# Staging the queries of an attention block in one step of 128 partitions, with 24 crossing transfers in place of 12, and a new order table

## The chip, the cores and the metric

One core of a Trainium2 chip runs one program with five instruction streams: TensorE (PE in the profile, with its weight loads as PEld), VectorE (DVE), ScalarE (ACT), GpSimd (POOL) and SyncE (SP). SP only issues DMAs here, all of the kernel's. Each stream is executed in the order in which it was written; the streams wait for each other through semaphores. The metric is device microseconds of one execution. The kernel before takes 738.09 us (median of 3 runs, 735.95 to 739.26).

## The reference

```python
def _A_ref(x, wqkv, wo):            # x: 1 x 2048 x 512
    H = 32; Dh = D // H; W = 256    # 32 heads of 16, window of 256
    qkv = (x @ wqkv).reshape(B, S, 3, H, Dh) ...
    scores = jnp.einsum("bhqd,bhkd->bhqk", q, k) * (Dh ** -0.5)
    mask = (idx[:, None] - idx[None, :] >= 0) & (idx[:, None] - idx[None, :] < W)
    p = _softmax(jnp.where(mask, scores, -1e9), axis=-1)
    o = jnp.einsum("bhqk,bhkd->bhqd", p, v)
    return o ... @ wo
def _B_ref(x, w_gate, w_up, w_down):    # 512 -> 1376 -> 512
    return (_sigmoid(x @ w_gate) * (x @ w_up)) @ w_down

h = x + _A_ref(_layernorm(x), wqkv, wo)
h2 = h + _B_ref(_layernorm(h), w_gate, w_up, w_down)
```

Layernorm, attention over a causal window of 256 positions, a projection and a residual, then a second layernorm and a gated unit with its own residual. All of it is float32 data; the kernel multiplies float16 halves (a high and a low part) three times for one product, so that the result keeps nearly float32 accuracy.

## The kernel before

**Stages.** The 2048 rows are cut into 8 blocks of 256 (b = 0 to 7). Attention runs from the start to about 430 us, block after block, several blocks under way at once; the gated unit runs over 8 pairs of row tiles and fills TensorE from about 450 us to the end. Its weights are read, split into halves and combined during the attention, on DVE, ACT and POOL, written to DRAM (`wr<-chunk`) and read back into place when the attention's buffers come free.

**What one block does.** `do_ln` normalizes two row tiles (`normal`: statistics and `rs`, the scaled variance, on DVE at L585; `rs` to the power of -1/2 on POOL at L588; the scaling on DVE) and transposes them. `do_qk` multiplies by the query and key weights (L406) into a PSUM tile of the ring `mm`, which has two buffers, and evacuates it into a staging tile: a scaled high half (ACT or DVE, helper at L359 or L363) and then the low half, product less high half, on DVE at L720. `do_queries` (L745) and `do_keys` move the staged halves with DMAs across partitions into `SQ` and `SK`, the operands of the score products. `do_s` (L799) computes scores of a pair of heads for one row maximum each, `row_max` on DVE takes it (L784); the maxima go back through a transpose and two small DMAs (`mh`, `mt`, L811 and L815) into `SQ` as extra rows. `do_st` (L853, L854, L855, L864) computes the transposed scores, ACT takes the exponential (L829), POOL cuts the triangles (L837, L842), `do_pv` (L890) multiplies by the values, ACT or DVE and DVE evacuate (`RH`), a DMA transpose and POOL bring the rows back (`RT`, `OS`), and `do_wo` multiplies by the output weights (L406).

**The staged queries.** Query columns are packed so that a row of a staging tile holds data for one of two positions, u = 0 or 1, beside each other in the stacked operand `SQ`: partitions 0 to 63 belong to u = 0, 64 to 127 to u = 1, and the other position has to hold zeros. The staging tile `sq` therefore has a place for both u in each row, was set to zeros once, and the evacuation writes 64 partitions to their u = 0 places in one instruction and the other 64 to their u = 1 places in a second one. For each of the 16 evacuations (8 blocks, two each) this makes two high-half and two low-half instructions. For each of 4 pairs of heads p, three DMAs (c = 0, 1, 2: the high half twice, the low half once) then pick every fourth partition, 32 rows of 4096 bytes each, 12 transfers a block.

**What sets the order.** Every operation is a step of a generator; the list `ORDER` names, step by step, which generator goes on and on which of the allowed engines. It was found by a search beforehand. A step that can run on one of several engines (the high halves, the subtractions) takes the one that the number names. So the table fixes the stream of each engine word for word, SP's with all DMAs too, and a transfer stands in SP's queue behind whatever the table put ahead of it.

Of the kernel before, what the change touches and what calls it, by code (L numbers as in the profile page):

```python
# [35 lines left out]
P = 128  # L36
# [300 lines left out]
def tile_block(ctx, tc, x, wqkv, wo, wg, wu, wd, out):  # L337
# [119 lines left out]
    for i in range(2):  # L457
        (G if i else V).memset(stage[i][0].rearrange("p h j i u t -> p (h j i u t)").bitcast(F32), 0.0)
# [1104 lines left out]
```

## Time and profile before

| | |
|---|---|
| median of 3 runs | 738.09 us |
| profiled execution, its own time | 739.39 us |
| its span, first to last instruction | 737.6 us |
| DVE busy | 621.1 us |
| ACT busy | 465.7 us |
| POOL busy | 368.7 us |
| TensorE clock granted | 1.00 of full speed throughout |
| DMA issues on SP | 538 |

The profiled execution lies 1.30 us above the median. Busy time is the union of an engine's records. A matmul's record starts when it starts, but its end is modelled, so that matmuls that follow each other overlap in the records; short waits between two of them do not show as idle time. "Idle before" in a row is the time in which the engine did nothing before these instructions, and the arrow names what ended it. DMA-issuing instructions of SP have durations, but are not counted as busy.

### The profile page before, as it was taken

Reading aid. Unit: us, or ns where it says so; the run is one execution under the profiler, and the core shown is the slowest. Engines: PE = TensorE matmul, PEld = TensorE weight load, DVE = VectorE, ACT = ScalarE, POOL = GpSimd, SP = SyncE. Lnnn points to the kernel's source line nnn. Section 1 sums busy time; section 2 is a strip of 40 time slices with the busy share of each in tenths; the row PEclk is TensorE's granted clock in tenths of the full one; section 3 lists DMA queues with packets and bytes.
Section 4 is the critical chain, followed back from the end, with each engine's and each line's share of the span. In section 5 each row is a group of like instructions: output and inputs, shape, how many; then the busy total and the mean of one; then the engine's idle time right before and its main releaser. Section 6 shows DMA issues by size and latency. Waiting matters only on the chain.

```text
span 737.6 us, 19193 instructions
## 1 busy us (share of the span) xinstructions
PE 723.5 (98%) x7008; PEld 501.8 (68%) x7008; DVE 621.1 (84%) x1870; ACT 465.7 (63%) x846; POOL 368.7 (50%) x451
## 2 busy tenths in 40 slices
PE   9999999999999999999999899999999999999997
PEld 5686877777776777786665454576666565766476
DVE  8999999998999999999999889986486767675752
ACT  5967989778898877899788777643233333233320
POOL 2553656545656574666685443455432544344250
PEclk9999999999999999999999999999999999999999
DMA  8797784978648878669889999866537575545453
GB/s 312 185 245 229 176 188 115 183 189 162 174 125 168 184 188 191 161 186 183 233 186 212 256 253 300 192 117 137 95 80 135 102 143 94 113 93 97 93 131 102
DMA packets 216031, 123.63 MB, mean 168 GB/s; under 512 B 174912, under 2 KB 189504, under 8 KB 215936
## 3 DMA queue, kind: packets, MB, share of 16 engines
q1 hardware_dynamic: 215936, 122.40, 72.2%
q8 instruction: 55, 0.90, 0.5%
q14 instruction: 40, 0.33, 0.2%
HBM read 46.17 MB, written 21.92 MB: 92 GB/s over the span
## 4 chain that ended last, share of the span: by engine, by line
PE 85%; DVE 5%; DMA 4%; ACT 3%; issue 2%; POOL 0%; SPq 0%; DVEq 0%; ACTq 0%; POOLq 0%
PE mmp L406 18%; PE sp L1201 15%; PE mmp L1378 12%; PE pvp L890 9%; PE sp L799 8%; PE stp L1201 7%; PE pvp L1201 3%; PE stp L864 3%; PE stp L854 3%; PE stp L853 2%; PE stp L855 2%; PE mmp L700 1%; PE mmp L1384 1%; DVE junk L784 1%; DMA wr<-chunk 1%
## 5 line engine op out<-in xcount | busy, mean ns | idle before, releaser
L784 DVE CUSTOM_DVE_ANT_0 junk<-sp,mask 128x320 uint8<-128x320 f32 (+4 forms) x512 | 215.8, 464 | 16.5 <-PE sp L799 13.8
L829 ACT ACTIVATE pa<-stp,kappa 128x512 f32<-128x512 f32 (+1 forms) x256 | 154.2, 645 | 28.3 <-PE stp L855 25.5
L1201 PEld LDWEIGHTS <-x 128*128 128x128 f16 x1008 | 98.1, 98 | 87.6 <-DMA x<-hl 0.9
L799 PE MATMUL sp<-SK,SQ 96*128 96x192 f16 (+3 forms) x960 | 127.5, 232 | 1.6 <-DVE mq L784 0.8
L799 PEld LDWEIGHTS <-SQ 96*128 96x128 f16 x960 | 79.6, 97 | 28.1 <-issue 9.7
L406 PE MATMUL mmp<-xT,W 128*128 128x256 f16 x672 | 97.1, 272 | 0.3
L829 ACT ACTIVATE pb<-stp,kappa 128x512 f32<-128x512 f32 x128 | 82.9, 686 | 18.0 <-PE stp L864 16.5
L1201 PE MATMUL sp<-W,x 128*128 128x512 f16 (+1 forms) x420 | 88.2, 349 | 0.0
L837 POOL TENSOR_SCALAR_AFFINE_SELECT pa<-pa 128x1024 f32<-128x1024 f32 x56 | 62.2, 1111 | 31.9 <-ACT pa L829 31.9
L359 ACT ACTIVATE SQ<-SQ 128x512 f16<-128x512 f32 (+3 forms) x65 | 34.0, 534 | 57.5 <-DVE SQ L1285 13.0
L406 PEld LDWEIGHTS <-W 128*128 128x128 f16 x672 | 60.5, 97 | 8.2 <-DVE sq L720 0.6
L842 POOL TENSOR_SCALAR_AFFINE_SELECT pb<-pb 128x512 f32<-128x512 f32 x64 | 41.2, 645 | 45.1 <-ACT pb L829 45.0
L890 PE MATMUL pvp<-pa,VT 128*17 128x128 f32 (+1 forms) x1408 | 62.5, 307 | 0.0
L854 PE MATMUL stp<-SQ,SK 100*128 100x256 f16 x224 | 59.6, 270 | 0.0
L366 POOL TENSOR_TENSOR SQ<-SQ,SQ 128x512 f16<-128x512 f32 (+3 forms) x41 | 38.5, 945 | 38.3 <-DVE SQ L361 21.3
L855 PE MATMUL stp<-SQ,SK 100*128 100x128 f16 x256 | 55.4, 218 | 0.4 <-ACT pb L829 0.3
L842 POOL TENSOR_SCALAR_AFFINE_SELECT pa<-pa 128x512 f32<-128x512 f32 x64 | 41.5, 652 | 23.5 <-ACT pa L829 23.3
L890 PEld LDWEIGHTS pvp<-pa,VT 128*17 128x17 f32 x1408 | 37.7, 97 | 22.7 <-issue 3.3
L406 PE MATMUL mmp<-WO,oT 128*128 128x512 f16 x192 | 51.0, 379 | 1.1 <-DMA oT<-whl 0.8
L853 PE MATMUL stp<-SQ,SK 100*128 100x128 f16 x224 | 49.2, 220 | 2.6 <-ACT pa L829 1.8
L406 PE MATMUL mmp<-W,xT 128*128 128x512 f16 x192 | 49.7, 378 | 0.0
L864 PE MATMUL stp<-SQ,SK 100*128 100x256 f16 x256 | 47.4, 272 | 1.2 <-ACT pa L829 1.2
(231 smaller groups left out, 1506.4 us busy)
## 6 DMA issues: line engine op xcount, KB each, us to landing
SQ<-sq SPq DMA_DIRECT2D x96, 128.0 KB
wr<-chunk SPq DMA_DIRECT2D x28, 256.0 KB
SK<-mem SPq DMA_DIRECT2D x16, 384.0 KB
chunk<-in_wd_dram SPq DMA_DIRECT2D x20, 256.0 KB
X<-in_x_dram SPq DMA_DIRECT2D x16, 256.0 KB
mem<-sk SPq DMA_DIRECT2D x8, 512.0 KB
out_dram<-X SPq DMA_DIRECT2D x16, 256.0 KB
W<-wr SPq DMA_DIRECT2D x7, 512.0 KB
```

The lines of the kernel that those rows point to most:

```text
L406: PE.matmul(ps, a_of(a, k), b_of(b, k), start=(k == 0 and i == 0), stop=(k == n - 1 and i == 2))
L784: V.tensor_tensor_reduce(out=junk[:, c0:], in0=ps[:, c0:], in1=mask[:, c0:], scale=1.0, scalar=-3.0e38, op0=ALU.add, op1=ALU.max, accum_ou ...
L799: PE.matmul(ps[:, col:col + k1 - k0], q, SK[0:96, (2 * a + hf) % 5, 4 * (p % 2) + j, k0:k1], start=True, stop=True)
L829: S.activation(dst, a, AF.Exp, scale=kappa)
L842: G.affine_select(out=p, in_=p, pattern=[[0, 4], [1, 128]], compare_op=ALU.is_ge, fill=0.0, base=0, channel_multiplier=-1)
L853: PE.matmul(a[:, 0:128], ks(k0, g, j), qs(b, g, j, 0, 128), start=True, stop=True)
L854: PE.matmul(a[:, 128:384], ks(k0 + 1, g, j), qs(b, g, j, 0, 256), start=True, stop=True)
L855: PE.matmul(a[:, 384:512], ks(k0 + 3, g, j), qs(b, g, j, 128, 256), start=True, stop=True)
L864: PE.matmul(a[:, u, :], ks(k0 + 2, g, j + u), qs(b, g, j + u, 0, 256), start=True, stop=True)
L890: PE.matmul(ps[32 * j:32 * j + 17, u, q0:q1], VT[:, kt % 6, 8 * j + g, :], w[:, j, c:c + q1 - q0], start=first, stop=last, skip_group_chec ...
L1201: PE.matmul(ps, X2[p % 2][part][:, (a * COUNT[part] + at) * 2 + k, :], operand(c, j)[:, b, k, :], start=first and k == 0 and i == 0, stop= ...
L1378: PE.matmul(ps, hT[p, c, r][:, a, half * kinds[c] + i, :], W["d"][2 * c + i][:, b, j, :], start=fresh and c == 0 and i == 0 and n == 0, st ...
```

## The change

The staging tile becomes one flat row of 64 + 2 x 2048 elements a partition. All 128 partitions are evacuated by one instruction a half, always to the u = 0 place of the row's second part (from element 64 on). The place for u is now made by the transfer: for u = 0 it reads 2048 elements from element 64 of the row, for u = 1 from element 0, so that the same data appear 64 elements later, behind zeros. Each transfer takes 16 rows, and there are 24 a block in place of 12; the bytes stay the same.

```diff
-        stage[i] = pool.tile([P, 2, 4, 4, 2, 64], F16, name=f"sq{i}"), ...
+        stage[i] = pool.tile([P, 64 + 4 * 2 * 512], F16, name=f"sq{i}"), ...
...
-        times = 2 - c
...
         if c:
...
         else:
-            parts = [(ps[64 * u:64 * u + 64].rearrange("r j (i t) -> r j i t", t=64),
-                      [dst[64 * u:64 * u + 64, h, 2 * jj:2 * jj + 2, :, u, :] for h in range(2)],
-                      sc["x" + nm][64 * u:64 * u + 64] if raw else float(2.0 ** -20)) for u in range(2)]
-        for x, (hi, _), f in parts:
-            copy(hi, x, f)
+            src = ps.rearrange("r j (i t) -> r (j i) t", t=64)
+            hi, lo = (dst[:, 64:].rearrange("r (h s u t) -> r h s u t", h=2, u=2, t=64)[:, h, 8 * jj:8 * jj + 8, 0, :] for h in range(2))
+        copy(hi, src, f)
...
-        for x, (hi, lo), f in parts:
-            V.scalar_tensor_tensor(lo, x, f, hi, op0=ALU.mult, op1=ALU.subtract)
+        V.scalar_tensor_tensor(lo, src, f, hi, op0=ALU.mult, op1=ALU.subtract)
...
         for c in range(3):
-            nc.sync.dma_start(SQ[b % 2][32 * c:32 * c + 32, 4 * p:4 * p + 4]...,
-                              stage[int(b == 1)][0][p:P:4, c // 2]...)
+            at = 64 + c // 2 * 2048
+            for u in range(2):
+                nc.sync.dma_start(SQ[b % 2][32 * c + 16 * u:32 * c + 16 * u + 16, 4 * p:4 * p + 4]...,
+                                  stage[int(b == 1)][0][64 * u + p:64 * u + 64:4, at - 64 * u:at - 64 * u + 2048])
```

Two smaller edits come with it. In `normal`, all row tiles but the first two compute `rs` on POOL, just ahead of the power that was there before. And the last low half made from a loaded weight chunk may now be made on POOL too, as a scaling in place and a subtraction:

```diff
-        V.tensor_scalar(rs, mv[:, 1:2], EPS, float(2.0 ** -shift), op0=ALU.add, op1=ALU.mult)
+        if early:
+            V.tensor_scalar(rs, mv[:, 1:2], EPS, float(2.0 ** -shift), op0=ALU.add, op1=ALU.mult)
...
+        if not early:
+            G.tensor_scalar(rs, mv[:, 1:2], EPS, float(2.0 ** -shift), op0=ALU.add, op1=ALU.mult)
         G.tensor_tensor(out=rs, in0=rs, in1=nhalf, op=ALU.pow)
...
+    def rest(lo, x, w, hi):
+        if plan.on == POOL_:
+            G.tensor_scalar(x, x, w, None, op0=ALU.mult)
+            subtract(lo, x, hi)
+        else:
+            V.scalar_tensor_tensor(lo, x, w, hi, op0=ALU.mult, op1=ALU.subtract)
...
 ORDER = [
-    3203, 7427, 7427, 7427, 771, 6659, 3331, 1027, 7811, 640, ...
```

The new table chooses POOL for four such low halves. TensorE executes the same 7008 matmuls in nearly the same order; the other streams are reordered throughout.

The first place shown is DVE's stream at the first of the two query evacuations of block 7. `sq_119` is the staging tile, `mmp` the PSUM tile of the product, `chunk<-X,sg` a low half of a gate weight, `junk,mq` a row maximum (an instruction and the read of its result). Before:

```order
L1088 SCALAR_TENSOR_TENSOR chunk<-X,sg,chunk 128x512
L720 SCALAR_TENSOR_TENSOR sq_119<-mmp,sq_119 64x8x64 x2
L1088 SCALAR_TENSOR_TENSOR chunk<-X,sg,chunk 128x512
L784 ISA junk,mq<-sp,mask 128x320
L784 ISA mq 128x1
```

The same place in DVE's stream of the changed kernel, where the table also put the high half on DVE (`whl` is a half of the attention's output):

```order
L368 TENSOR_SCALAR sq_119<-mmp 128x8x64
L366 CAST whl<-OS 128x512
L792 ISA junk,mq<-sp,mask 128x320
L792 ISA mq 128x1
L726 SCALAR_TENSOR_TENSOR sq_119<-mmp,sq_119 128x8x64
```

Two low halves of 64 partitions became one of 128, and the two weight halves that stood around them stand elsewhere.

The second place is SP's stream in block 6, around the last query transfers (`SQ_73<-sq_119`) of its first pair of heads; `SK<-mem` brings keys, `oT<-whl` and `RT<-RH` are transposes of the attention's output, `wr<-chunk` writes split weights. Before:

```order
L745 DMA SQ_73<-sq_119 32x2048
L736 DMA SK<-mem 96x2048
L745 DMA SQ_73<-sq_119 32x2048 x2
L666 DMA_TRANSPOSE oT<-whl 128x8x128
L745 DMA SQ_73<-sq_119 32x2048
L1099 DMA wr_5270<-chunk 256x1x512
L1099 DMA wr_5849<-chunk 256x1x512
L745 DMA SQ_73<-sq_119 32x2048
L1099 DMA wr_5882<-chunk 256x1x512
L745 DMA SQ_73<-sq_119 32x2048 x2
L913 DMA_TRANSPOSE RT<-RH 128x8x128
```

The same stretch of SP's stream in the changed kernel:

```order
L753 DMA SQ_73<-sq_119 16x2048 x2
L742 DMA SK<-mem 96x2048
L1121 DMA wr_5742<-chunk 256x1x512
L753 DMA SQ_73<-sq_119 16x2048
L675 DMA_TRANSPOSE oT<-whl 128x8x128
L753 DMA SQ_73<-sq_119 16x2048
L1121 DMA wr_5290<-chunk 256x1x512
L753 DMA SQ_73<-sq_119 16x2048 x8
L921 DMA_TRANSPOSE RT<-RH 128x8x128
L1121 DMA wr_5106<-chunk 256x1x512
```

Between the keys and the transpose `RT<-RH`, 10 half-size transfers stand where 6 stood; the last three of the first pair are among the eight in a row.

More of the change, by code (lines that the diff above doesn't have):

```diff
@@ L455, in tile_block @@
     for i, pool in enumerate((qk, wp)):
-        stage[i] = pool.tile([P, 2, 4, 4, 2, 64], F16, name=f"sq{i}"), pool.tile([P, 2, 4, B], F16, name=f"sk{i}")
+        stage[i] = pool.tile([P, 64 + 4 * 2 * 512], F16, name=f"sq{i}"), pool.tile([P, 2, 4, B], F16, name=f"sk{i}")
     for i in range(2):
-        (G if i else V).memset(stage[i][0].rearrange("p h j i u t -> p (h j i u t)").bitcast(F32), 0.0)
+        (G if i else V).memset(stage[i][0].bitcast(F32), 0.0)
     V.tensor_copy(identh, ident)
@@ L576, in normal @@
     def normal(t, key, ring, tile, shift, n_of=1, ln1=False):
-        e, n = yield {DVE_: 1.0}, key, ["ln"]
+        early = ln1 and t < 2
+        e, n = yield {DVE_: 1.0 if early else 0.87}, key, ["ln"]
         src = xs[t][0] if ln1 else home(t)
@@ L584, in normal @@
         rs = small.tile([P, 1], F32, name="rs")
-        V.tensor_scalar(rs, mv[:, 1:2], EPS, float(2.0 ** -shift), op0=ALU.add, op1=ALU.mult)
+        if early:
+            V.tensor_scalar(rs, mv[:, 1:2], EPS, float(2.0 ** -shift), op0=ALU.add, op1=ALU.mult)
         both = "xn" in C["alts"]
-        e, = yield {POOL_: 1.1 if both else 0.62}, [e]
+        e, = yield {POOL_: 1.1 if both else 0.62 if early else 0.75}, [e]
+        if not early:
+            G.tensor_scalar(rs, mv[:, 1:2], EPS, float(2.0 ** -shift), op0=ALU.add, op1=ALU.mult)
         G.tensor_tensor(out=rs, in0=rs, in1=nhalf, op=ALU.pow)
@@ L705, in do_qk @@
                 mm3(ps[:, j, :], lambda a, k: W1[:, a, k, c0:c0 + P], lambda a, k: xT[b][:, a, k, :], k, KT)
-        times = 2 - c
-        e, = yield alt("qk", ACT_, ACT=0.52 * times + 0.16 * (times - 1), DVE=0.62 * times + 0.16 * (times - 1)), [e] + ["xq"] * raw
+        e, = yield alt("qk", ACT_, ACT=0.52, DVE=0.62), [e] + ["xq"] * raw
+        f = sc["xq"] if raw else float(2.0 ** -20)
         dst = stage[int(b == 1)][c]
         if c:
-            parts = [(ps, [dst[:, h, 2 * jj:2 * jj + 2, :] for h in range(2)], sc["x" + nm] if raw else float(2.0 ** -20))]
+            src, hi, lo = ps, *(dst[:, h, 2 * jj:2 * jj + 2, :] for h in range(2))
         else:
-            parts = [(ps[64 * u:64 * u + 64].rearrange("r j (i t) -> r j i t", t=64),
-                      [dst[64 * u:64 * u + 64, h, 2 * jj:2 * jj + 2, :, u, :] for h in range(2)],
-                      sc["x" + nm][64 * u:64 * u + 64] if raw else float(2.0 ** -20)) for u in range(2)]
-        for x, (hi, _), f in parts:
-            copy(hi, x, f)
-        e, = yield {DVE_: 0.63 * times + 0.157 * (times - 1)}, [e]
+            src = ps.rearrange("r j (i t) -> r (j i) t", t=64)
+            hi, lo = (dst[:, 64:].rearrange("r (h s u t) -> r h s u t", h=2, u=2, t=64)[:, h, 8 * jj:8 * jj + 8, 0, :] for h in range(2))
+        copy(hi, src, f)
+        e, = yield {DVE_: 0.63}, [e]
         plan.free("mm", n, e)
-        for x, (hi, lo), f in parts:
-            V.scalar_tensor_tensor(lo, x, f, hi, op0=ALU.mult, op1=ALU.subtract)
+        V.scalar_tensor_tensor(lo, src, f, hi, op0=ALU.mult, op1=ALU.subtract)
         plan.mark(("qk", b, c, jj), e)
@@ L743, in do_queries @@
         for c in range(3):
-            e, = yield {DMA_: 0.645}, needs, [], 0.85
-            nc.sync.dma_start(SQ[b % 2][32 * c:32 * c + 32, 4 * p:4 * p + 4].rearrange("r j i u t -> r j (i u t)"),
-                              stage[int(b == 1)][0][p:P:4, c // 2].rearrange("r j i u t -> r j (i u t)"))
+            at = 64 + c // 2 * 2048
+            for u in range(2):
+                e, = yield {DMA_: 0.645}, needs, [], 0.42
+                nc.sync.dma_start(SQ[b % 2][32 * c + 16 * u:32 * c + 16 * u + 16, 4 * p:4 * p + 4].rearrange("r j i u t -> r (j i u t)"),
+                                  stage[int(b == 1)][0][64 * u + p:64 * u + 64:4, at - 64 * u:at - 64 * u + 2048])
         plan.mark(("queries", b, p), e)
@@ L1009, in do_amax, with lower, halves @@
             plan.mark(("scale", nm), t)
-    def halves(hi, lo, x, w, cols, needs):
+    def lower(cols, last):
+        costs = dict(DVE=Port(cols / 960 + 0.13))
+        if last:
+            costs["POOL"] = Port(2 * (cols * 0.0021 + 0.1))
+        return costs
+    def rest(lo, x, w, hi):
[4 more added lines that the diff above has]
+            V.scalar_tensor_tensor(lo, x, w, hi, op0=ALU.mult, op1=ALU.subtract)
+    def halves(hi, lo, x, w, cols, needs, last):
         t, = yield alt("phi", ACT_, ACT=cols / 1200 + 0.187, DVE=Port(cols / 1920 + 0.075)), needs
         copy(hi, x, w)
-        t, = yield {DVE_: Port(cols / 960 + 0.13)}, [t]
-        V.scalar_tensor_tensor(lo, x, w, hi, op0=ALU.mult, op1=ALU.subtract)
+        t, = yield lower(cols, last), [t]
+        rest(lo, x, w, hi)
         return t
@@ L1028, in do_split @@
             hi, lo = (W["l"][:r, h, :] for h in range(2))
-            t = yield from halves(hi, lo, x, sc["sd"][:r], D, [t])
+            t = yield from halves(hi, lo, x, sc["sd"][:r], D, [t], True)
             plan.free("chunk", place, t)
@@ L1045, in part @@
             hi, lo = (W["d"][m][:, h, j:j + n, :].rearrange("p j n -> p (j n)") for h in range(2))
-            t = yield from halves(hi, lo, x, sc["sd"], n * HALF, needs)
+            t = yield from halves(hi, lo, x, sc["sd"], n * HALF, needs, last is not None)
             plan.mark(("dpart", m, j), t)
@@ L1086, in part @@
             copy(hl[:, 0, :], x[i], sc[scale])
-            t, = yield {DVE_: Port(cols / 960 + 0.13)}, [t]
-            V.scalar_tensor_tensor(hl[:, 1, :], x[i], sc[scale], hl[:, 0, :], op0=ALU.mult, op1=ALU.subtract)
+            t, = yield lower(cols, last is not None), [t]
+            rest(hl[:, 1, :], x[i], sc[scale], hl[:, 0, :])
             plan.mark(("part", c, k, j), t)
```

449 rows, old and new, of the table ORDER are left out of this document.

## The prediction

> **What bounds the kernel now.** I read the head of the page, then the windows of the span, then TensorE's waits, then the groups of instructions by shape, and last SP's own timeline, because that is where the change adds work.
>
> ```profile
> span 737.6 us, 19193 instructions
> PE 723.5 (98%) x7008; PEld 501.8 (68%) x7008; DVE 621.1 (84%) x1870; ACT 465.7 (63%) x846; POOL 368.7 (50%) x451
> ```
>
> TensorE is busy for 723.5 of 737.6 us, so 14.1 us is all of its visible idle time. Where it lies is read from the windows; the columns are the stretch, its length, the busy us of PE, PEld, DVE, ACT and POOL with their instructions, the granted clock, the DMA engines' share and GB/s.
>
> ```profile
> 0.00:25.00 25.00, 23.36 (x97) 15.84 (x98) 21.41 (x52) 17.03 (x37) 7.92 (x16) 1.00 0.79 265
> 25.00:50.00 25.00, 23.32 (x207) 17.83 (x206) 24.22 (x93) 19.82 (x40) 16.42 (x20) 1.00 0.85 219
> 75.00:100.00 25.00, 24.28 (x311) 19.22 (x310) 24.24 (x106) 22.16 (x54) 14.65 (x21) 1.00 0.72 174
> 350.00:375.00 25.00, 24.61 (x342) 16.47 (x341) 24.00 (x82) 18.62 (x32) 16.72 (x21) 1.00 0.79 211
> 375.00:400.00 25.00, 23.27 (x290) 15.84 (x287) 24.38 (x88) 21.50 (x36) 16.36 (x21) 1.00 0.95 208
> 400.00:425.00 25.00, 22.26 (x241) 12.95 (x239) 21.46 (x42) 18.98 (x34) 13.95 (x17) 1.00 1.01 240
> 425.00:450.00 25.00, 24.07 (x176) 11.72 (x175) 22.94 (x42) 17.89 (x31) 10.48 (x12) 1.00 1.11 268
> 700.00:737.60 37.60, 33.80 (x283) 27.34 (x280) 16.32 (x32) 5.93 (x11) 10.86 (x13) 1.00 0.47 114
> ```
>
> The idle time of a window is its length less PE's busy time: 1.64 and 1.68 us in the first two, 0.72 at 75, then 0.39, 1.73, 2.74 and 0.93 from 350 to 450, and 3.80 in the last stretch. These make 13.6 of the 14.1. So the middle of the attention and the gated unit are bound by TensorE itself at a clock of 1.00, and the change, which adds and takes no matmul, can gain only in the first 50 us, around 75 to 100, and from 350 to 450, where the attention runs out while the gated unit's weights are still being made. The last 38 us hold nothing that it touches. One reserve: matmul ends are modelled, so short waits hide in the busy time; the visible 14.1 is a lower bound of what TensorE waits.
>
> What ended the idle time, by name (engine, result, line, what was waited for: us, times, longest):
>
> ```profile
> PE stp L853 <- ACT pa L829: 1.8, 2, 1.6
> PE stp L864 <- ACT pa L829: 1.2, 2, 1.0
> PE mmp L659 <- ACT xT L359: 1.1, 1, 1.1
> PE mmp L406 <- DMA oT<-whl: 0.8, 1, 0.8
> PE stp L853 <- ACT pb L829: 0.6, 2, 0.4
> PE stp L855 <- ACT pb L829: 0.3, 1, 0.3
> PEld L406 <- DVE sq L720: 0.6, 2, 0.3
> ```
>
> The exponentials on ACT (`pa`, `pb`) make 1.8 + 1.2 + 0.6 + 0.3 = 3.9 us. Of the low half that this change halves, only 0.6 us in two places is waited for directly.
>
> **The change part by part.** First the staging.
>
> ```profile
> L720 DVE SCALAR_TENSOR_TENSOR sq<-mmp,sq 64x512 f16<-64x512 f32 x28 | 19.2, 687 | 0.5 <-ACT sq L359 0.2
> L720 DVE SCALAR_TENSOR_TENSOR sk<-mmp,sk 128x512 f16<-128x512 f32 x14 | 9.5, 679 | 0.0
> L720 DVE SCALAR_TENSOR_TENSOR sq<-mmp,xq,sq 64x512 f16<-64x512 f32 x4 | 3.0, 750 | 0.1
> L359 ACT ACTIVATE sq<-mmp 64x512 f16<-64x512 f32 x28 | 16.5, 589 | 4.1 <-PE mmp L406 3.4 <-PE sp L799 0.6
> L359 ACT ACTIVATE sq<-mmp,xq 64x512 f16<-64x512 f32 x4 | 2.7, 682 | 1.4 <-DVE xq L398 1.3
> L359 ACT ACTIVATE sk<-mmp 128x512 f16<-128x512 f32 x12 | 7.0, 596 | 3.8 <-PE mmp L406 3.3 <-PE sp L799 0.2
> ```
>
> The keys show the price of the new form: 128 partitions take 679 ns where 64 take 687, and 596 against 589 on ACT. Halving the number halves the time. On DVE 32 low halves (19.2 + 3.0 = 22.2 us) become 16 (14 x 0.679 + 2 x 0.750 = 11.0): **-11.2 us**. On ACT 32 high halves (16.5 + 2.7 = 19.2 us) become 13, since the table puts 3 on DVE: at 0.596, 7.7 us, **-11.5 us**; DVE gets those 3 back, about +1.8 at the same price (estimate from ACT's row).
>
> ```profile
> L585 DVE TENSOR_SCALAR rs<-mv 128x1 f32<-128x1 f32 x32 | 4.9, 153 | 1.1
> L588 POOL TENSOR_TENSOR rs<-rs,nhalf 128x1 f32<-128x1 f32 x32 | 19.3, 602 | 33.0 <-DVE rs L585 32.9
> L1088 DVE SCALAR_TENSOR_TENSOR chunk<-X,sg,chunk 128x512 f16<-128x512 f32 x20 | 15.8, 804 | 0.0
> L366 POOL TENSOR_TENSOR X<-X 128x512 f32<-128x512 f32 x7 | 9.1, 1303 | 12.2 <-DVE X L1107 12.2
> ```
>
> Thirty of 32 `rs` leave DVE: 30 x 0.153 = 4.6 us, of which 14 (2.1 us) belong to the attention. Four weight low halves leave it too: 4 x 0.804 = 3.2 us. With them DVE loses 11.2 + 2.1 + 3.2 - 1.8 = 14.7 us before the end of the attention; but the new table puts value evacuations and weight halves on DVE that were on ACT or POOL, about ten of 0.6 (the 0.596 of ACT's row again), some 6 us. So **DVE's net is about -9 us**. POOL gains 30 small operations, whose price is not in the trace: above 0.153 (DVE's) and below 0.602 (the power of one column on POOL). I take 0.4, nearer to the POOL row, 12 us over the whole program; and 4 x 2 operations of 512 columns at up to 1.3, 10 us. POOL is busy for 50%, and in the windows from 350 on at most 16.7 of 25. Its new `rs` waits for the statistics where the power waited for `rs` before, so nothing new stands behind a wait: the triangles queued behind it, and `do_pv` behind those, wait no longer than by the operation itself. I cost POOL at nothing; if that cover goes, one layernorm in the open costs 0.6 at most, and the two weight halves that could meet a triangle 2.6: the end is +3.
>
> **What of it reaches the end.** DVE is busy for 24.0 and 24.4 of 25 us between 350 and 400, and 24.2 in both early windows, so microseconds taken from it are carried forward rather than lost in its own gaps. ACT idles for 3.5 to 7 us in each of the windows from 350, so that most of what is taken from it before 330 us, where its last query half stands, is lost in gaps ahead of the place at which TensorE waits for it.
> - First 50 us: the 1.1 us wait for `xT` (a copy on ACT) follows two early high halves saved (2 x 0.682), but those stood behind 1.3 us of waiting for `xq`. I take **-0.3**, ends 0 and -1.1.
> - Direct waits for the low half: one of the two instructions goes, **-0.5** of the 0.6.
> - DVE's 9 us in 350 to 450: idle there and at 75 is 0.72 + 0.39 + 1.73 + 2.74 + 0.93 = 6.5, less ACT's 3.9 leaves 2.6. I take **-2.5**. Ends: 0, if DMAs are what is late; -9.0, if all of DVE's relief lay on the path through hidden short waits.
> - ACT: a quarter of 3.9, **-1.0**; ends 0 and -3.9 (contained in DVE's -9.0, as both act on one place).
>
> Then what it adds: DMA issues.
>
> ```profile
> L745 SPq DMA_DIRECT2D SQ<-sq x96: 467/589/1725, 19.4 to 345.9; - x96
> SQ<-sq SPq DMA_DIRECT2D x96, 128.0 KB
> SK<-mem SPq DMA_DIRECT2D x16, 384.0 KB
> 356.92 3.91 DMA SK<-mem
> 282.61 1.20 SPq L815 DMA_DIRECT2D SQ<-mt  x2
> 289.04 1.11 SPq L745 DMA_DIRECT2D SQ<-sq  x2
> 298.19 1.26 SPq L913 DMA_TRANSPOSE RT<-RH  x1
> 299.08 0.30 PE L799 MATMUL sp<-SK,SQ 96*128 96x256 f16 x2
> ```
>
> 96 more issues at the median of 0.589 are **+56.5 us on SP**, spread over 19 to 346 us, and 7.1 us more in each block. The bytes and the rows of 4096 stay, so the 16 DMA engines get no more to move. A transfer of half as many rows may issue faster: the ends are 0.29 each (half) and 0.589. I take 0.589, as the row's own low of 0.467 is nearer to it. Is SP free for that? Not in the busiest stretch: from 282.61 to the transpose that starts at 298.19 there are 14 lines of the timeline, whose issue times sum to 14.2 of the 16.8 us to that transpose's end, nine of the issues being query transfers. Nine more at 0.589 are 5.3: the queue ends 14.2 + 5.3 - 16.8 = 2.7 us later. Behind it stand the transposes `RT<-RH`, the maxima's transfers and the weights written. Against that stands slack: the last transfer of block 6's first pair is the second of the pair at 289.04, issued by 290.15, and the first score product that reads it is at 299.08, 8.9 us later. A transfer of three times the size (keys, 384 KB) held up the chain for 3.91, so landing takes at most about that, which leaves 5.0 us of slack against a lateness of 2.7. I therefore take **+1.0** for all of SP, nearest to the case of a queue that is late but covered; ends 0 and +8.4, the price worked out in the last rival below.
>
> [...]
>
> Sum against the profiled execution's own 739.39: -0.3 - 0.5 - 2.5 - 1.0 + 1.0 = -3.3, that is 736.1. That execution lies 1.30 above the median, so the forecast is **734.8 us** as a median of runs, against 738.09.
>
> **The rivals.**
> - *DVE was the gate.* All of the 9.0 reaches the end, with -1.1 and -0.6 of the early waits and SP for nothing: 739.39 - 10.7 - 1.30 = 727.4; with the visible idle time alone (6.5 + 1.1 + 0.6 = 8.2) 729.9. For it: DVE at 24 of 25. Against it: from 400 to 450 DVE has 2 to 3.5 us free in each window while the DMA share is 1.01 and 1.11.
> - *Nothing arrives.* The late waits are for DMAs (`oT<-whl`; DMA share up to 1.11), and bytes are not saved; only the two direct waits go: 739.39 - 0.5 + 0.3 for POOL and SP - 1.30 = 737.9. That the change does not do what it says, because 128 partitions might cost twice 64, would end here too, but the keys' rows exclude it.
> - *SP's queue becomes the bound: slower.* Place: the query transfers of a block against its first scores. With all 7.1 us of a block ahead of its first scores, less the slack of 5.0, TensorE stands 2.1 us; with nine of the twelve ahead, as in the stretch, 5.3 - 5.0 = 0.3. The middle, 1.2, in blocks 1 to 7 (block 0 meets no backlog) is +8.4, and 2.1 in each would be 14.7. With the reliefs of 4.3, which lie at other places: 739.39 - 4.3 + 8.4 - 1.30 = 742.2. It decides from the point where a block's queue is later than 5.0 us; the stretch shows 2.7. For it: SP's issue share of 14.2 in 16.8. Against it: the table places each transfer anew, and SP's queue is only that full in stretches.
>
> **How the numbers follow.** The forecast case, a partial relief between 731 and 738, gets 0.50, of which 0.26 lies below 734.4; DVE as the gate 0.14; nothing arrives 0.14, of which 0.03 is faster than the bound and 0.11 within; SP as the bound 0.22, of which 0.06 falls within the bound and 0.16 beyond it, as its price spreads up to 14.7. A measurement of this kernel tells 0.5%, 3.7 us, from no change. Faster than 734.4: 0.26 + 0.14 + 0.03 = 0.43; within: 0.24 + 0.11 + 0.06 = 0.41; slower than 741.8: 0.16. The range takes in the ends of the sum: 727.4 below; 742.2 above, and with a share of POOL's 3 and of that spread 744.0; under one in ten lies beyond. The likeliest case's own range is 731 to 738.
>
> **What would show it.** In the changed profile the query low half should read 128x512, 16 times, some 680 ns, and DVE about 9 us less up to the last row maximum; a mean near 1300 ns would fell the first term. TensorE's idle time from 350 to 450 should fall from 5.8 to about 3; unchanged, nothing arrived; near nothing, DVE was the gate. The waits for the low half should be one short one or none. SP's query issues should be 192 at a median of 0.59; a median near 0.3 halves SP's load. If TensorE's waits name the query transfers at the scores, by microseconds and in several blocks, the last rival holds. I am wrong altogether if the new table moves idle time to a place that none of these rows shows, the gated unit from 450 on above all.

## The result, and the profile after

| | before | after |
|---|---|---|
| median | 738.29 us (4 runs, 735.95 to 739.26) | 749.79 us (4 runs, 747.69 to 751.66) |
| ratio after to before | | 1.0158 (95%: 1.0138 to 1.0177) |
| profiled execution, span | 737.6 us | 749.9 us |

The changed kernel is slower by 1.6%, some 11.5 us. The prediction was 734.8 us, with a range that ended at 744.0.

The head of the page after, with the same columns as before:

```profile
span 749.9 us, 19270 instructions
PE 727.1 (97%) x7008; PEld 501.7 (67%) x7008; DVE 609.7 (81%) x1840; ACT 452.2 (60%) x817; POOL 378.4 (50%) x476
```

DVE and ACT are busy for 11.4 and 13.5 us less, so the change does what it says. TensorE is idle for 749.9 - 727.1 = 22.8 us in place of 14.1, and its busy time grew by 3.6 us with the same matmuls. Where, is read from the windows of the changed kernel:

```profile
0.00:25.00 25.00, 22.42 (x104) 16.25 (x105) 21.38 (x50) 16.63 (x35) 11.60 (x21) 1.00 0.73 255
25.00:50.00 25.00, 22.42 (x190) 16.58 (x189) 21.97 (x81) 15.82 (x30) 16.43 (x23) 1.00 0.70 194
50.00:75.00 25.00, 23.17 (x198) 16.64 (x195) 20.40 (x111) 12.76 (x30) 10.06 (x9) 1.00 0.81 232
75.00:100.00 25.00, 24.57 (x308) 18.74 (x306) 24.25 (x104) 23.31 (x58) 14.35 (x22) 1.00 0.77 159
100.00:350.00 250.00, 245.63 (x3223) 186.74 (x3222) 227.26 (x821) 197.61 (x336) 151.53 (x184) 1.00 0.66 169
350.00:375.00 25.00, 22.41 (x249) 15.07 (x251) 19.99 (x76) 17.75 (x30) 16.08 (x21) 0.93 0.69 198
375.00:400.00 25.00, 24.56 (x339) 16.73 (x328) 24.31 (x86) 20.41 (x36) 19.54 (x25) 1.00 1.04 216
400.00:425.00 25.00, 24.81 (x271) 15.22 (x270) 23.32 (x61) 22.31 (x39) 13.22 (x17) 1.00 0.93 225
425.00:450.00 25.00, 22.80 (x219) 11.59 (x218) 19.98 (x40) 16.88 (x28) 12.95 (x18) 0.93 1.05 274
```

and, for the two stretches that were not shown of before:

```profile
50.00:75.00 25.00, 24.91 (x219) 18.27 (x217) 23.52 (x123) 17.77 (x40) 9.04 (x10) 1.00 0.85 238
100.00:350.00 250.00, 249.66 (x3264) 190.01 (x3262) 234.59 (x845) 211.22 (x363) 148.79 (x183) 1.00 0.76 172
```

Idle time in the first 100 us is 7.4 in place of 4.1, from 100 to 350 it is 4.4 in place of 0.3, from 350 to 450 it is 5.4 in place of 5.8, and the rest is 5.6 in place of 3.8. By 400 us the changed kernel has started 4587 matmuls and the kernel before 4712, so that equal windows do not hold equal work. Still, the stretch in which I expected the gain idles as long as it did, and the middle of the attention, which TensorE filled before, has waits now. DVE and ACT are emptier there, and the DMA engines too (0.66 in place of 0.76): all of them wait for something else. Of the 5.6 us of the rest, 1.8 lie between 450 and 700 us, in the gated unit, where TensorE shows no idle time before. TensorE's largest waits name it:

```profile
PE sp L807 <- DMA SK<-mem: 4.6, 3, 2.5
PE stp L861 <- ACT pa L837: 2.8, 3, 2.2
PE sp L807 <- DVE mq L792: 2.7, 7, 0.8
PE stp L861 <- DMA SQ<-mt: 1.2, 1, 1.2
```

Scores wait for keys (`SK<-mem`), three times, and for row maxima on DVE (`mq`); transposed scores wait for exponentials (`pa`) and for the maxima's transfer (`SQ<-mt`). No transfer of queries is among them. Why the keys are late at 204 us, SP's timeline shows (start, duration, line, what, how many):

```profile
192.37 8.88 SPq L753 DMA_DIRECT2D SQ<-sq  x12
201.29 1.40 SPq L742 DMA_DIRECT2D SK<-mem  x1
```

Twelve query transfers stand in a row ahead of the keys in this view, which begins at 193 us: 8.88 us. The chain of waits goes back from the score through 5.35 us for the keys to the issues of the last six query transfers, the first of them at 197.39 us, and TensorE stands for 1.73:

```profile
200.66 0.59 SPq L753
...
201.29 5.35 DMA SK<-mem
```

```profile
206.68 0.19 PE L807 MATMUL sp<-SK,SQ 96*128 96x64 f16 x1 [1.73 <-DMA SK<-mem]
```

The staging itself came out as worked out. The rows of the staged queries, and of their transfers with size and median time to landing:

```profile
L753 SPq DMA_DIRECT2D SQ<-sq x192: 492/587/1647, 17.5 to 359.3; - x192
L726 DVE SCALAR_TENSOR_TENSOR sq<-mmp,sq x14: 680/688/692, 36.7 to 333.7; 128x512 f16<-128x512 f32 x14
L364 ACT ACTIVATE sq<-mmp x11: 576/597/597, 39.1 to 332.1; 128x512 f16<-128x512 f32 x11
SQ<-sq SPq DMA_DIRECT2D x192, 64.0 KB, 2.7
```

A low half of 128 partitions takes 688 ns, and a transfer of half the size takes SP the same time to issue, by the median: 587 ns against 589.

### The profile page after: what moved, and what is told of

Same layout as the page of the kernel before. It is cut to its first block, busy times and chain, and to the rows that moved or that the text cites. A ratio compares the mean times of both kernels' runs of the same rounds, so it can differ in the third digit from the quotient of the medians.

```text
span 749.9 us, 19270 instructions
## 1 busy us (share of the span) xinstructions
PE 727.1 (97%) x7008; PEld 501.7 (67%) x7008; DVE 609.7 (81%) x1840; ACT 452.2 (60%) x817; POOL 378.4 (50%) x476
## 4 chain that ended last, share of the span: by engine, by line
PE 72%; DVE 10%; DMA 8%; issue 4%; ACT 3%; SPq 1%; POOL 1%; DVEq 0%; ACTq 0%; POOLq 0%
PE sp L1223 13%; PE mmp L411 12%; PE mmp L1400 11%; PE pvp L898 9%; PE sp L807 7%; PE stp L1223 6%; PE stp L872 3%; PE pvp L1223 3%; PE stp L862 2%; DMA SK<-mem 2%; DVE junk L792 2%; PE mmp L709 2%; DMA chunk<-in_wu_dram 2%; PE stp L861 2%; PE stp L863 1%
## 5 line engine op out<-in xcount | busy, mean ns | idle before, releaser
L792 DVE CUSTOM_DVE_ANT_0 junk<-sp,mask 128x320 uint8<-128x320 f32 (+3 forms) x512 | 216.4, 464 | 26.5 <-PE sp L807 24.5
L837 ACT ACTIVATE pa<-stp,kappa 128x512 f32<-128x512 f32 (+1 forms) x256 | 155.8, 645 | 37.2 <-PE stp L863 32.5
L807 PE MATMUL sp<-SK,SQ 96*128 96x128 f16 (+3 forms) x960 | 128.6, 233 | 8.2 <-DMA SK<-mem 4.6
L411 PE MATMUL mmp<-xT,W 128*128 128x256 f16 x672 | 98.1, 272 | 0.0
L371 POOL TENSOR_TENSOR SQ<-SQ,SQ 128x512 f16<-128x512 f32 (+3 forms) x45 | 40.4, 901 | 59.3 <-ACT SQ L364 35.8
L411 PEld LDWEIGHTS <-W 128*128 128x128 f16 x672 | 60.1, 97 | 10.0 <-issue 3.2
L850 POOL TENSOR_SCALAR_AFFINE_SELECT pb<-pb 128x512 f32<-128x512 f32 x64 | 43.4, 680 | 37.8 <-ACT pb L837 36.2
L861 PE MATMUL stp<-SQ,SK 100*128 100x128 f16 x224 | 49.4, 221 | 4.2 <-ACT pa L837 2.8
L411 PE MATMUL mmp<-WO,oT 128*128 128x512 f16 x192 | 51.8, 383 | 0.0
L411 PE MATMUL mmp<-W,xT 128*128 128x512 f16 x192 | 50.6, 385 | 0.0
```

Source lines behind the costliest of these rows:

```text
L411: PE.matmul(ps, a_of(a, k), b_of(b, k), start=(k == 0 and i == 0), stop=(k == n - 1 and i == 2))
L792: V.tensor_tensor_reduce(out=junk[:, c0:], in0=ps[:, c0:], in1=mask[:, c0:], scale=1.0, scalar=-3.0e38, op0=ALU.add, op1=ALU.max, accum_ou ...
L807: PE.matmul(ps[:, col:col + k1 - k0], q, SK[0:96, (2 * a + hf) % 5, 4 * (p % 2) + j, k0:k1], start=True, stop=True)
L837: S.activation(dst, a, AF.Exp, scale=kappa)
L850: G.affine_select(out=p, in_=p, pattern=[[0, 4], [1, 128]], compare_op=ALU.is_ge, fill=0.0, base=0, channel_multiplier=-1)
L861: PE.matmul(a[:, 0:128], ks(k0, g, j), qs(b, g, j, 0, 128), start=True, stop=True)
```

## The experiments

Theory **Q**: SP's queue. Each issue takes SP 0.59 us, SP works in order (the twelve above end at 201.25 us, the keys start at 201.29), and 96 more make what stands behind them late. Theory **T**: the new order table costs the time, whatever the number of issues. Theory **D**: 192 transfers of 64 KB load the DMA engines more than 96 of 128 KB. Each run was timed beside the kernel before; the ratios are to that. The medians of before lay between 737.5 and 738.6.

**The transfers alone, in the old kernel.**

```diff
         for c in range(3):
             e, = yield {DMA_: 0.645}, needs, [], 0.85
-            nc.sync.dma_start(SQ[b % 2][32 * c:32 * c + 32, ...], stage[...][0][p:P:4, c // 2]...)
+            for u in range(2):
+                nc.sync.dma_start(SQ[b % 2][32 * c + 16 * u:32 * c + 16 * u + 16, ...], stage[...][0][64 * u + p:64 * u + 64:4, c // 2]...)
```

> The kernel before with its own order and staging; only each query transfer of 32 rows is issued as two of 16 rows, back to back in the same place, 192 issues in place of 96. Theory Q (SP's queue: doubled issues at 0.587 us make everything behind them late): 742 to 750 us, with TensorE waits on transfers that the kernel before does not have. Theory T (the new order table itself costs the 11.5 us, whatever the number of issues): within 1.5 us of the kernel before, 737 to 740.

Measured: 754.53 us, ratio 1.022 (1.0198 to 1.0241). With the old table and the old staging, splitting the transfers costs more than the whole change, and more than the range that I had given for Q. As the whole cause, T falls. TensorE's waits are of the kind seen after:

```profile
PE sp L800 <- DMA SK<-mem: 6.4, 5, 1.8
PE sp L800 <- DVE mq L785: 3.8, 6, 1.1
```

What the issues used up shows in SP's own waits, which are waits at the head of its queue. From 100 to 350 us, before:

```profile
SPq L913 <- DVE mq L784: 16.1, 5, 6.2
SPq L913 <- DVE RH L902: 12.6, 5, 5.0
SPq L736 <- PE sp L799: 10.6, 5, 6.3
```

and with the split transfers (the same transposes `RT<-RH` and keys):

```profile
SPq L914 <- DVE mq L785: 10.9, 4, 6.0
SPq L736 <- PE sp L800: 6.9, 3, 6.3
SPq L914 <- DVE RH L903: 4.6, 2, 3.0
```

The three fell from 39.3 to 22.4 us; a fourth large row, the maxima's transposes behind `mq`, from 11.9 to 8.8. The time that SP waits for others is what it can still give; issue times in this stretch, summed over SP's timeline, rose from 159 us of 250 to 197 in the changed kernel, which has as many split transfers.

**The changed kernel with half the issues.**

```diff
             for u in range(2):
                 e, = yield {DMA_: 0.645}, needs, [], 0.42
-                nc.sync.dma_start(SQ[b % 2][32 * c + 16 * u:32 * c + 16 * u + 16, ...], stage[...][0][64 * u + p:64 * u + 64:4, at - 64 * u:at - 64 * u + 2048])
+                if u:
+                    nc.sync.dma_start(SQ[b % 2][32 * c:32 * c + 32, ...], stage[...][0][p:P:4, at:at + 2048])
```

> The changed kernel with its own table and one-step staging, but of each pair of query transfers only the second is issued, for all 32 rows, and reads without the shift: 96 issues, the same bytes, and the zeros between the two positions of a query are left out, so that scores are computed from other data. Theory Q: 738 to 742, the waits for keys at 68, 205 and 354 us gone. Theory T: 747 to 751.

Measured: 738.61 us, ratio 1.0010 (1.0000 to 1.0021). Undoing the issues alone, with the new table, the new staging and the work moved to POOL in place, takes all the loss away. It also shows what the reliefs bring under the new table: nothing at the end. DVE is busy for 608.0 us there (621.1 before), ACT for 452.2, and the time is that of before. From 350 to 450 us TensorE idles for 5.2 us (5.8 before), but from 450 to 700 us, in the gated unit, for 1.4 us where the kernel before does not idle. These are two waits for DVE, 0.6 us for `SQ` and

```profile
PE mmp L1401 <- DVE X L1372: 0.8, 1, 0.8
```

which the changed kernel has too, at the same size. TensorE's largest wait of this run is where I had put the gain:

```profile
426.63 0.22 PE L862 MATMUL stp<-SQ,SK 100*128 100x128 f16 x1 [3.52 <-ACT pa L838]
```

and the chain ahead of it leads, past ACT, to transfers:

```profile
406.81 6.14 DMA wr<-chunk
...
417.76 7.01 DMA x<-hl
424.85 1.15 ACT hl L1189 x2
426.00 0.58 ACT pa L838
```

The exponential `pa` stands in ACT's queue behind two writes of the second layernorm's halves (`hl`), and these wait until the transfer `x<-hl` has read the buffer, 7.01 us after its issue. The kernel before has the same two pieces in its chain:

```profile
406.55 8.15 DMA wr<-chunk
...
420.53 5.35 DMA x<-hl
```

Together 13.5 us then and 13.2 now: the relief of DVE and ACT did not shorten them.

**The staging alone, in the old kernel with split transfers.** The edit is the one of the change to `do_qk` and the stage tile, with both shifted transfers issued in one step of the old table.

> The kernel before with its own order table, one-step staging of 128 partitions, and the two shifted transfers issued back to back where one was. Against the run with only the transfers split it shows what the staging alone is worth under the old table. If DVE and ACT relief reaches the end as I predicted (2.5 + 1.0 + 0.8 us): 3 to 5 us less than that run. If it is lost in gaps: within 1.5 us of it. Theory T further says 734 to 738, theory Q 739 to 748.

Measured: 755.41 us, ratio 1.0247 (1.0222 to 1.0272), against 754.53 without it. A second time the staging brings nothing to the end, though here SP's queue, which it does not relieve, holds both runs. The clean case, the one-step staging with 96 transfers and the old table, was not run.

**Keys ahead of queries.** In the list, four numbers were moved ahead by 26 to 55 places, each past query transfers; the one of block 4:

```diff
-    26643, 30083, 30083, 30083,
+    26643, 30083, 29699, 30083, 30083,
...
-    26655, 22659, 29699, 27651, 25475,
+    26655, 22659, 27651, 25475,
```

> The changed kernel with four entries of its table moved, all of key transfers: in blocks 1, 4 and 7 a transfer of keys (and in block 7 its copy to DRAM) goes ahead of the query transfers that stood before it; nothing else moves. If the place of the keys behind runs of query transfers is the mechanism (theory Q in its sharp form): the waits of 0.5, 1.9 and 2.6 us and the slow clock after the last go, 743 to 746 us. If those waits only show a lateness that has another cause: 748 to 751.

Measured: 749.69 us, ratio 1.0160 (1.0147 to 1.0174): no change. A miss of the sharp form. The keys of block 4 go out at 194.85 us in place of 201.29, and no wait for keys is left in this profile, but

```profile
194.85 0.51 SPq L514 DMA_DIRECT2D SK<-mem  x1
```

```profile
PE sp L579 <- DVE mq L564: 6.1, 7, 2.8
```

the maxima are waited for in their place, 6.1 us where it was 2.7. So the place of the keys alone does not make the loss. What makes the maxima late in this run was not followed further.

**Issues without bytes.** To the run with half the issues, 96 tiny transfers were added:

```diff
             for u in range(2):
                 e, = yield {DMA_: 0.645}, needs, [], 0.42
+                if not u:
+                    nc.sync.dma_start(dram.tile([16, 16], F16, name=f"tiny{b}{p}{c}", bufs=1), stage[...][0][p:64:4, at:at + 16])
                 if u:
```

> The run with 96 query transfers and the new table (738.6 us), plus 96 transfers of 16 rows of 32 bytes to DRAM scratch, one at each place in the table at which the first half of a pair stood: as many issues on SP as in the changed kernel, but only 48 KB more to move and no more rows for the queries themselves. As there, the zeros between the positions of a query are left out. If SP's issue time is the price (theory Q): 747 to 752, as the changed kernel. If it is the DMA engines that 192 transfers of 64 KB load (theory D): 738 to 741.

Measured: 751.48 us, ratio 1.0184 (1.0154 to 1.0215). Adding 48 KB in 96 transfers costs what splitting the 96 into 192 of 64 KB costs. As a matter of bytes, D falls; Q holds in its plain form, the time SP takes for an issue, by the median 590 ns for 512 bytes here and 587 ns for 64 KB in the changed kernel:

```profile
L754 SPq DMA_DIRECT2D tiny<-sq x96: 477/590/1418, 17.4 to 354.3; - x96
```

A price that each transfer has on the DMA engines whatever its size would give the same time; this run does not separate it from SP's issue. The chain shown above, through SP's issues to the keys, and the next run speak for SP.

**Half the queries from ACT.**

```diff
-                nc.sync.dma_start(SQ[b % 2][32 * c + 16 * u:..., ...], ...)
+                (nc.scalar if u else nc.sync).dma_start(SQ[b % 2][32 * c + 16 * u:..., ...], ...)
```

> The changed kernel with the second transfer of each pair (u = 1) issued by ACT in place of SP, at the same place in the table: the same 192 transfers, SP with the load that it had before the change. Theory Q: SP's 10 us come back, less what 96 issues cost ACT, which is busy for some 80% of the attention: if an issue takes ACT under 0.1 us, 739 to 742; at 0.59, as on SP, 745 to 755 with waits on ACT's exponentials in place of those on keys. Theory D: no better than 749.

Measured: 754.42 us, ratio 1.0212 (1.0185 to 1.0240). The transfers are the same 192, and with half of them off SP no wait for keys is left in the list, which is what Q says and a price on the DMA engines does not. Waits for ACT stand in their place:

```profile
L753 ACTq DMA_DIRECT2D SQ<-sq x96: 499/500/1729, 18.0 to 359.6; - x96
```

```profile
PE stp L861 <- ACT pa L837: 7.3, 8, 2.2
PE stp L872 <- ACT pa L837: 1.7, 3, 1.2
PE stp L861 <- ACT pb L837: 1.6, 2, 1.2
```

An issue takes ACT 0.500 us, 96 of them 48 us, and in the changed kernel ACT is already busy for 198 of 250 us from 100 to 350 us. In the list of what waited for the instructions of the staged queries one `pa` on ACT stands with 2.7 us, and TensorE's waits for `pa` at L861 rose from 2.8 to 7.3 us. One by one an issue is small beside its transfer, in the changed kernel 0.59 us against a median of 2.7 us to landing for 64 KB. Added up it is not: 96 issues are 56 us of a queue that other transfers wait in.

**Does SP limit the kernel before?** A third of the old query transfers from ACT:

```diff
-            nc.sync.dma_start(SQ[b % 2][32 * c:32 * c + 32, ...], ...)
+            (nc.scalar if c == 1 else nc.sync).dma_start(SQ[b % 2][32 * c:32 * c + 32, ...], ...)
```

> The kernel before with one third of its query transfers, the second copy of the high half (32 of 96), issued by ACT in place of SP. If SP's queue limits the kernel before already, by the same slope (17 us for 96 issues): 733 to 737. If the kernel before is past the knee, with slack that covers its 538 issues: 737 to 741, more where ACT pays for the issues.

Measured: 739.33 us, ratio 1.0011 (0.9998 to 1.0024). Taking 32 issues off SP gains nothing; what ACT pays for them is not separated from it.

**How many issues are too many.** Four runs split only some of the old transfers, with the edit of the first experiment under a condition: `c == 2` (4 more a block), `p in (0, 2)` (6), `c != 1` (8), and `b > 3` (12, in the last four blocks alone).

> The kernel before with only the low-half transfers (c = 2) split in two: 32 more issues, spread evenly over the blocks, in place of 96. With 32 fewer the time did not move (739.3), with 48 more in the last four blocks it rose by 12, with 96 more by 17. If the loss grows in proportion from the load before on: 742 to 745. If there is a knee between: 738 to 741.

> The kernel before with the transfers of two of the four pairs of heads (p = 0 and 2) split in two in every block: 48 more issues, 6 a block, as many as in the run that put 12 more into each of blocks 4 to 7 and rose by 12 us. If the number of issues counts: about 748 to 751. If their density in a block counts, with a knee between 4 and 12 more a block: 739 to 743.

> The kernel before with the first high-half and the low-half transfers (c = 0 and 2) split in two in every block: 64 more issues, 8 a block. With 4 more a block nothing was lost, with 12 more 17 us. If the loss grows in a straight line from a knee at 4: about 747; if most of it comes with the last four: 739 to 743.

> The kernel before with the transfers split in two in blocks 4 to 7 alone: 48 more issues in place of 96, all after 190 us. The run with all 96 lost 8.4 us by then and 6.7 us after it. If the loss is made where the issues are, about 744 to 747; if the early lateness (block 0 and 1, before 60 us) is the larger part and later blocks only follow, 739 to 741.

| more issues | a block | median us | ratio to before (95%) |
|---|---|---|---|
| 32 | 4 | 738.94 | 1.0012 (1.0000 to 1.0023) |
| 48 | 6 | 740.86 | 1.0042 (1.0026 to 1.0058) |
| 64 | 8 | 742.76 | 1.0056 (1.0035 to 1.0077) |
| 96 | 12 | 754.53 | 1.0220 (1.0198 to 1.0241) |
| 48 | 12, blocks 4 to 7 | 750.70 | 1.0160 (1.0132 to 1.0189) |

The loss is not proportional: the first four a block cost some 1 us, the next four some 3 us, the last four 12. And 48 issues cost 3 us when spread evenly and 12 when they stand in four blocks. I had expected 744 to 747 for the last row, too little. What fits these rows is density against slack: how many issues fall into a stretch, and how much free time SP has there. The rows do not split the same transfers, so that a part of the steps may be due to which ones they are.

**Could another table mend it?** 115 of the 192 transfers were moved later in the changed kernel's list, each by up to 9 us of TensorE's work; one of block 4 (30083, where 29955 and 29827 are moved transfers of its other pairs of heads):

```diff
-    22275, 7939, 30083, 4867, 51968,
+    22275, 29955, 7939, 4867, 51968,
...
-    27423, 27419, 22531, 22531, 26883, 26639,
+    27423, 27419, 22531, 22531, 29955, 29827, 30083, 29827, 26883, 26639,
```

> The changed kernel with 115 of its 192 query transfers moved later in the table, by up to 9 us of TensorE work, each at least 7 us of it ahead of the scores that read it, so that keys, maxima, transposes and loads that stood behind them go first. The number of issues is the same, nothing else moves. If the loss is one of places in the queue, which a table could mend: 742 to 746. If it is the number of issues, and whatever goes first makes something else late: 748 to 753.

Measured: 777.9 us, ratio 1.0541 (1.0517 to 1.0565), worse than either theory said. The row of query transfers ahead of block 4's keys did not shorten but grew to seventeen. The moved queries became late themselves, and the keys stayed so:

```profile
PE sp L579 <- DMA SK<-mem: 8.0, 4, 3.6
PE sp L579 <- DVE mq L564: 6.2, 8, 1.9
PE sp L579 <- DMA SQ<-sq: 4.1, 3, 1.5
```

Not all of the loss is waiting: TensorE's busy time grew to 739.0 us (727.1 in the changed kernel), with a granted clock of 0.98 over the run. The run shows that my rule for moving them was bad, not that no table could do better: the new table, with the small work that it moves to POOL, is at 749.79 us itself better than the old one with the same transfers and staging, 755.41.

## Why the prediction was wrong

- **The staging's arithmetic was right.** Halving the instructions halved their time: 688 ns for 128 partitions, where 64 had taken 687, DVE's and ACT's busy time down by 11.4 and 13.5 us.
- **The reliefs (-0.3 - 0.5 - 2.5 - 1.0) did not arrive.** The run with half the issues has all of them and stands at 1.0010 of before. Up to 450 us little of them shows (0.6 us less idle from 350 to 450), and TensorE loses 1.4 us to two new waits for DVE in the gated unit, where the prediction had said that new idle time would mean that it was wrong altogether. The rival "nothing arrives" had this half right: the late waits of the attention lead back to transfers (6.14 and 7.01 us in the chain). That these transfers hold the time there is read from the chain; no run shortened them. I had argued that an engine busy for 24 of 25 us carries its relief forward; being busy is not being waited for, and the wait rows, with 0.6 us for this work, had said so.
- **The step that failed is SP's term, +1.0.** It measured about +11 (749.79 against 738.61 with half the issues). I had the price of an issue right (0.587 us), and the queue as the place to look, where I worked out a lateness of 2.7 us in one stretch. Then I set it against the slack of one transfer, the first pair's queries, and took it for covered. The waits came at what stands behind the queries on SP, first of all the keys (4.6 us of waits, where the kernel before has none that shows); I had named maxima and transposes without working out their slack, and the keys not at all. And I took one stretch for the whole: from 100 to 350 us SP issues for 197 of 250 us, 159 before, so that it has less free time to make up a lateness before the next block. That the lateness is handed on from block to block is argued from this, not shown by a run.
- **The slower rival had the mechanism, but the wrong place and too low a price.** It put TensorE's waits at the query transfers and +8.4 us; they came at keys and maxima, and when the keys were taken ahead, most of all at maxima.
- **The order table** was suspect by its size and is not guilty of the 11 us: of the 17 us that the split costs under the old table, the new one with its work on POOL gave back about 5. The 1.4 us of new waits in the gated unit came with it or with that work; which of the two was not tried.

The runs show no version that beats both kernels: fewer issues on SP than before bring nothing, the staging brought nothing where it was tried, and TensorE is busy for 98% of the kernel before.

## What to carry to other kernels

An engine that only issues DMAs is an engine: add up its issue times in each stretch, as for the others, before a change adds to their number, since an issue took as long for 512 bytes as for 64 KB here (590 and 587 ns). Look for the slack of everything that stands behind the added issues in that queue, not of the added transfers alone; the queue's own waiting time is the reserve, and here the first four issues more a block used some of it up (the three rows of SP's waits fell from 39.3 to 32.3 us) at no cost that shows clearly (a ratio of 1.0012). And a relief counts only where a wait row names the relieved work; an engine busy for 97% of a stretch, as DVE from 350 to 400 us before, with hardly a wait on it may give microseconds that nobody collects.

## What was not expected of the hardware

After some waits TensorE's clock was lower. In the changed kernel the windows behind the waits at 354.4 (2.48 us, for keys) and 434.8 (2.16 us, for `pa`):

```profile
358.00:362.00 4.00, 4.00 (x30) 2.61 (x29) 2.55 (x9) 2.56 (x4) 0.00 (x0) 0.77 0.38 118
436.00:440.00 4.00, 3.02 (x14) 1.47 (x14) 2.23 (x7) 3.80 (x7) 1.84 (x3) 0.79 1.15 345
```

These are averages over 4 us. Narrower windows of the same trace show a granted clock of 0.50 from 356.42 to 359.83 us and from 438.34 to 441.75 us, 3.41 us each, and 1.00 in the 3.41 us ahead of each and behind it. TensorE was busy for 2.96 and 3.41 us of them. Three products of L411 took 1.28 us in the second, and 0.65 us just ahead of it. If all of this work would have taken half the time at a clock of 1.00 (an estimate from these), they make 3.2 of the 3.6 us by which TensorE's busy time grew. In the run with half the issues no such loss stands behind the wait of 3.52 us:

```profile
424.00:428.00 4.00, 1.37 (x10) 0.88 (x10) 2.38 (x7) 2.96 (x6) 0.20 (x1) 1.00 1.08 376
428.00:432.00 4.00, 4.00 (x60) 2.15 (x60) 1.44 (x3) 3.80 (x5) 4.00 (x6) 1.00 1.08 248
```

So the length of the wait alone does not decide it: 2.16 us stand ahead of one drop, and 3.52 us ahead of none. Nor was TensorE idle throughout just ahead of the two drops: in those 3.41 us it was busy for 1.38 and 1.35 us. In the run with all transfers split under the old table the window from 25 to 50 us reads 0.93, though no wait in its list of TensorE's waits is longer than 1.8 us. In the run with blocks 4 to 7 split that list has a wait of 2.5 us for keys, and the granted clock was 1.00 over the run. What decides it stays open.
